# One 64 KB-row load for the keys of two pairs, and the diagonal sums placed behind the next pair's scores, in a one-token decoder block

## The chip, the cores and the metric

The kernel runs on one core of a Trainium2 chip. The metric is the device time of one execution in microseconds (us), the median of several executions. TensorE is called PE, VectorE DVE, ScalarE ACT, GpSimd POOL and SyncE SP, as in the profile.

## What is computed

One token (`x`, 512 wide) goes through a layer-normed attention block over a cache of 16384 keys and values with 8 kv heads, 4 query heads to each, and then through a small mixer and MLP block. Nearly all of the data is the cache: 33.6 MB of keys and as much of values.

```
q = (layernorm(x) @ wq).reshape(32 heads, 128)
scores = einsum("bhqd,bhkd->bhqk", q, repeat(k_cache, 4)) * 128**-0.5
o = einsum("bhqk,bhkd->bhqd", softmax(scores), repeat(v_cache, 4))
h = x + o.reshape(4096) @ wo
...
def B(x):                                  # x = layernorm(h), S = 1
    hs = concat(shifted quarters of gelu(layernorm(x) @ w1)) @ w2
    x1 = x + hs
    return x1 + gelu(layernorm(x1) @ w3) @ w4
return h + B(layernorm(h))
```

With one token, the shifted quarters are all padding, so `hs` is zero and `w1` and `w2` are not read.

## The kernel before

The kv heads are worked in four pairs (`PAIRS`); this text counts them 0 to 3. The 128 partitions hold two heads of 64 rows each, and a partition's part of one pair is 256 keys of 128 numbers, 64 KB. Keys come into `kb`, which holds one pair and has two halves, `kb[0]` and `kb[1]`, of 32 KB per partition (128 keys each). `load_keys(j, y)` loads half `y` of pair `j`. Values come into `vb`, one pair in one load (`load_values`), and `vb` first holds `wq`.

Keys arrive with the head's numbers along the free axis, so DVE transposes each half in 32 x 32 blocks into `kt` (`transpose_keys`, L655). `kt` holds one half, in eight pieces; the `cuts` say at which pieces a transpose begins, so that `(0, 4)` means two transposes of four pieces. PE multiplies the pieces with the query (`scores`, four matmuls per piece, L666) and adds into two PSUM banks. A transpose into a piece of `kt` has to wait until PE has read what half 0 left there.

Then comes `softmax`: the row maximum (`mx`, DVE), its spread over the partitions with a matmul (L683), Exp on ACT, and the transpose of the probabilities to `pt` (L695). In that time `unread(16)` gives PE 16 matmuls whose result nobody reads (L508). `sums` (L713) adds up the denominators, `values` multiplies `pt` with `vb` (L706, 64 matmuls). `gather` takes from its result in `O_ps[0]` the sums that belong to each head (four DVE operations, L722 and L725), a small matmul (L728), and one DVE multiply by the reciprocal denominators into `o_m` (L730). This is called the diagonal sums here. After it, the next pair's query is copied to `qn` (L740) and its keys are transposed.

At the end stand the product with `wo` (L775), the second layer norm, `w3` and `w4` (L828 and L514). `wo` is loaded into `kb[0]`, `w3` and `w4` into `kb[1]`, when the last pair's halves have been read.

Every load but that of `x` goes out on SP's queue, in program order. A load waits on SP until the last readers of its buffer are done. Engines run their own streams; a small planner (`Program`) derives from reads and writes which semaphores each waits for. DVE counts up one semaphore with each operation that is needed elsewhere (a transpose of n pieces counts n), and PE, whose work on the pairs is one loop with registers (`_tensor`), waits for values of that counter. This is why every pair must add the same to it (`worth`, `SEEN`, `ROUND`).

Of the kernel before, what the change touches and what calls it, by code (L numbers as in the profile page):

```python
# [7 lines left out]
BF16 = mybir.dt.bfloat16  # L8
I32 = mybir.dt.int32
# [347 lines left out]
NCH = D // 128  # L357
# [4 lines left out]
WO = ((0, 20), (20, 32))  # L362
VP = 1

SEEN, ROUND = 47, 28
W3 = ((0, 4),)
W4 = ((0, 8), (8, 13), (13, 14))
PAIRS = HKV // 2
RPARTS = 6
QPAD = 4 * 7  # L370
KP = 8 * DH
# [9 lines left out]
def bass_sequential_preLN__gqa_block_cached__mixer_s_mlp__decode_kernel(  # L381
# [13 lines left out]
    with ExitStack() as ctx:  # L395
        sb = lambda name, shape, dt: ctx.enter_context(nc.sbuf_tensor(name, shape, dt))
        ps = lambda name, shape, dt: ctx.enter_context(nc.psum_tensor(name, shape, dt))
        P = Program(nc, ctx)
# [21 lines left out]
        zd = sb("zd", [128, 32], FP32)  # L420
# [9 lines left out]
        nm = sb("nm", [128, 2, REP], FP32)  # L430
        nmh = sb("nmh", [128, 2 * REP], FP32)
        bias = sb("bias", [128, 1], FP32)
# [3 lines left out]
        od = sb("od", [128, 128], FP32)  # L436
        osum = sb("osum", [128, D], FP32)
        den = sb("den", [32, 1], FP32)
# [12 lines left out]
        kb_all = sb("kb", [128, 256 * DH], BF16)  # L451
        kb = [kb_all[:, i * 128 * DH:(i + 1) * 128 * DH] for i in range(2)]
        vb = sb("vb", [128, 256 * DH], BF16)
        kt = sb("kt", [128, 128 * DH], BF16)
        wq_sb, wo_sb = vb, kb[0]
        w3_sb = kb[1][:, 0:NCH * FM].rearrange("p (k f) -> p k f", k=NCH)
        w4_sb = kb[1][:, NCH * FM:2 * NCH * FM].rearrange("p (m c) -> p m c", m=NHC)
# [6 lines left out]
        m_ps, n_ps = mn_ps[:, 0:256], mn_ps[:, 256:512]  # L464


        def load(name, dst, src, key, by="SP", also=()):
            P.op(by, lambda e: e.dma_start(dst, src), w=[key, *also], dma=name)

        def pair_rows(src, j):  # L470
            return src[0, 2 * j:2 * j + 2].rearrange("g (u t) d -> (g u) (t d)", u=64)

        def load_keys(j, y):
            n = 128 * DH
            load(f"k{y}", kb[y][:, :], pair_rows(A_k_cache, j)[:, y * n:(y + 1) * n], ("r", y, 0),
                 also=[("r", y, i) for i in range(1, RPARTS)])

        def load_values(j):
            n = 256 // VP * DH
            if j < PAIRS - 1:  # L480
                load("v", vb[:, :], pair_rows(A_v_cache, j), ("v", 0),
                     also=[("v", x) for x in range(1, VP)] + [("landed", x) for x in range(VP)])
                P.op("POOL", lambda e: e.nop(), r=[("v", 0)], w=[("landed", x) for x in range(VP)],
                     worth=ROUND if j else SEEN, own="v")
                return
            for x in range(VP):
                load(f"v{x}", vb[:, x * n:(x + 1) * n], pair_rows(A_v_cache, j)[:, x * n:(x + 1) * n], ("v", x),
                     also=[("landed", x)])
            for x in range(VP):
                P.op("POOL", lambda e: e.nop(), r=[("v", x)], w=[("landed", x)], worth=ROUND, own="v")  # L490


        def dve(fn, r=(), w=(), bank=(), own=None):
            return P.op("DVE", fn, r, w, bank, own=own)

        def act(fn, r=(), w=(), bank=(), own=None):
            return P.op("ACT", fn, r, w, bank, own=own)
# [4 lines left out]
        def pe(fn, r=(), w=(), bank=(), also=(), times=None, many=1):  # L502

            return P.op("PE", fn, r, w, bank, also=also, times=times, many=many)

        def unread(times):
            field = qb[:, :, :, :].rearrange("p a j q -> p (a j q)")
            P.op("PE", lambda e: e.matmul(O_ps[1][:, :], field[:, 0:128], field[:, 0:512], start=True, stop=True),  # L508
                 r=["qb"], bank=[("O", 1)], times=times)
# [53 lines left out]
        def inverse_roots(i, ns):  # L563
# [36 lines left out]
            r=["ident_f", "x4"], w=["quarter"])  # L600
# [47 lines left out]
                qcol[lo:hi, :, :, 0].rearrange("p n (j h) -> p n j h", h=REP)), r=["qcol"], w=["qb"])  # L648


        def transpose_keys(y, cuts):
            for t, n in zip(cuts, [b - a for a, b in zip(cuts, [*cuts[1:], 8])]):
                view = lambda x, t=t, n=n: x[:, :].bitcast(I32).rearrange("p (x l w) -> p x (l w)", x=2, l=64)[
                    :, :, t * 512:(t + n) * 512]
                P.op("DVE", lambda e, view=view: e.transpose(view(kt), view(kb[y])),  # L655
                     r=[("r", y, i) for i in range(RPARTS)], w=[("kt", t + i) for i in range(n)], worth=n)

        def key_piece(at, n):
            part = kt[:, :].rearrange("p (x f) -> p x f", x=2)[:, :, bass.ds(at, KP)]
# [18 lines left out]
        def softmax(j):  # L678

            dve(lambda e: e.tensor_reduce(mx[:, :], s_all, AX.X, ALU.max), r=[("s", 0), ("s", 1)], w=["mx"], **both)  # L680
            dve(lambda e: e.tensor_scalar(mxd[:, :], ident_f[:, :], mx[:, 0:1], None, ALU.mult),  # L681
                r=["mx", "ident_f"], w=["mxd"])
            pe(lambda e: e.matmul(m_ps[:, 0:128], mean4[:, :], mxd[:, :], start=True, stop=True),  # L683
               r=["mxd", "mean4"], w=["m"], bank=["mn"])
            dve(lambda e: e.tensor_reduce(nm[:, :, :], m_ps[:, 0:128].rearrange("p (g n h) -> p g h n", g=2, h=REP),
                                          AX.X, ALU.min), r=["m"], w=["nm"], bank=["mn"])
            dve(lambda e: e.scalar_tensor_tensor(nmh[:, :], nm[:, :, :].rearrange("p g h -> p (g h)"),  # L687
                                                 32 * D * SCALE, zd[:, :].rearrange("p (n d) -> p n d", d=4)[:, :, 0],
                                                 ALU.mult, ALU.mult, accum_out=bias[:, :]),
                r=["nm", "zd"], w=["nmh", "bias"])  # L690
            act(lambda e: e.activation(p_sb[:, :], s_all, ACTF.Exp, bias=bias[:, 0:1], scale=float(SCALE),  # L691
                                       accum_out=acc[:, :]),
                r=[("s", 0), ("s", 1), "bias"], w=["p", "acc"], **both)
            for g in range(2):
                dve(lambda e, g=g: e.transpose(pt[64 * g:64 * g + 64, :, :, g, :], p_sb[64 * g:64 * g + 64, :]),  # L695
                    r=["p"], w=["pt"])
# [14 lines left out]
        def sums(j):  # L711

            pe(lambda e: e.matmul(n_ps[0:32, 32:33], zd[:, :], acc[:, :], start=True, stop=True),  # L713
               r=["acc", "zd", "pt"], w=["n"], bank=["mn"])
            dve(lambda e: e.reciprocal(den[:, :], n_ps[0:32, 32:33]), r=["n"], w=["den"], bank=["mn"])  # L715
        def gather(j):

            O, key = O_ps[0], ("O", 0)
            for c in range(4):
                block = O[:, c * 128:(c + 1) * 128]  # L720
                if c == 0:
                    dve(lambda e, block=block: e.tensor_scalar(od[:, :], block, rowc[:, 0:1], None, ALU.mult),  # L722
                        r=[key, "rowc"], w=["od"], bank=[key])
                else:
                    dve(lambda e, block=block, c=c: e.scalar_tensor_tensor(  # L725
                        od[:, :], block, rowc[:, c:c + 1], od[:, :], ALU.mult, ALU.add),
                        r=[key, "rowc", "od"], w=["od"], bank=[key])
            pe(lambda e: e.matmul(A_ps[0:32, 0:128], zo[:, :], od[:, :], start=True, stop=True),  # L728
               r=["od", "zo"], w=["A"], bank=["A"])
            dve(lambda e: e.scalar_tensor_tensor(  # L730
                o_m[32 * j:32 * j + 32, :, :], A_ps[0:32, 0:128].rearrange("p (d r) -> p d r", d=4), den[:, 0:1],
                maskdd[0:32, :].unsqueeze(2).to_broadcast([32, 4, 32]), ALU.mult, ALU.mult),
                r=["A", "den", "maskdd"], w=["o_m"], bank=["A"])

        load_values(0)
        for j in range(PAIRS):
            P.part()
            clear()
            P.part("query", j)
            dve(lambda e, j=j: e.tensor_copy(qn[:, :, :], qb[:, :, j, :]), r=["qb", ("s", 0), ("s", 1)], w=["qn"])  # L740
            for y in range(2):
                P.part("half", j, y)
                transpose_keys(y, (0, 4) if j < PAIRS - 1 else range(8) if y else (0, 1, 2, 4, 6))
                scores(j, y)
                if j < PAIRS - 1:
                    load_keys(j + 1, y)
            P.part("middle", j)
            softmax(j)
            unread(16)
            sums(j)  # L750
            values(j)
            P.part("rest", j)
            gather(j)
            if j < PAIRS - 1:
                load_values(j + 1)
        P.part()
        act(lambda e: e.activation(scr[0:1, 1:2], mean4[0:1, 0:1], ACTF.Gelu_apprx_tanh), r=["mean4"], w=["scr"])
        for n, (lo, hi) in enumerate(WO):
# [114 lines left out]
```

## Time and profile before

| | |
|---|---|
| median of 3 runs | 189.70 us (189.63 to 189.85) |
| the profiled execution's own time | 189.84 us |
| its span (first to last instruction) | 188.5 us |
| PE busy | 131.4 us (70%) |
| DVE busy | 116.6 us (62%) |
| ACT busy | 13.7 us (7%) |
| read from HBM | 79.17 MB, 420 GB/s over the span |
| mean granted PE clock | 0.919 |

The profile is one execution. Its span leaves out what lies before the first and after the last instruction, so the execution's own time is 1.34 us longer. A row of the timeline gives start, duration, engine, line, operation and tiles, and in brackets the idle time before it and what ended it. A row of grouped instructions gives, behind the bar, busy time and mean nanoseconds of one. In the view of stretches, the columns are busy time and count by engine, then the granted PE clock as a share, the DMA engines' busy share, and GB/s; packets are counted where they start, so a short stretch can show over 100%.

### The profile page before, as it was taken

To read this page: it belongs to the slowest core of one execution; us is meant where nothing else is said; L and a number is where in the kernel's file an instruction comes from. 1 tells how busy PE (TensorE), PEld (TensorE's weight loads), DVE (VectorE), ACT (ScalarE), POOL (GpSimd) and SP (SyncE) were. 2 spreads that over 40 slices of the span, in tenths; PEclk is the share of its full clock that TensorE was granted. 3 is DMA by queue.
4 is the path that set the end of the run, shared out by engine and by line. 5 is a ranking of instruction groups with operands and counts; after the bars stand their busy time and mean duration, and the time that the engine had idled before them with its cause. 6 is when DMAs were issued, how large, how long until landed. Compare 5 with 4: busy or idle time off the path is not lost.

```text
span 188.5 us, 2406 instructions
## 1 busy us (share of the span) xinstructions
PE 131.4 (70%) x767; PEld 51.1 (27%) x767; DVE 116.6 (62%) x139; ACT 13.7 (7%) x21; POOL 4.6 (2%) x8
## 2 busy tenths in 40 slices
PE   0109902978879419888794198887947999696783
PEld 0103401333324203333242033332422333133321
DVE  5740599699152597891525978915259997543165
ACT  3000100000040000000400000004000000320012
POOL 8100000000000000000000000000000000000000
PEclk9999985599999966999999669999996999999789
DMA  6999999999799999988999999997999999969994
GB/s 227 468 417 445 445 445 445 445 445 445 334 445 445 445 556 417 431 348 382 424 445 445 445 445 445 445 445 341 438 445 445 556 445 431 431 297 404 423 414 162
DMA packets 2895, 79.19 MB, mean 420 GB/s; under 512 B 334, under 2 KB 462, under 8 KB 718
## 3 DMA queue, kind: packets, MB, share of 16 engines
q1 hardware_dynamic: 2886, 79.17, 97.7%
q8 instruction: 1, 0.02, 0.0%
q10 hardware_dynamic: 8, 0.00, 0.0%
HBM read 79.17 MB, written 0.00 MB: 420 GB/s over the span
## 4 chain that ended last, share of the span: by engine, by line
PE 51%; DVE 35%; DMA 6%; issue 6%; ACT 0%; SPq 0%; DVEq 0%; ACTq 0%
DVE kt L655 25%; PE banks L666 20%; PE banks L508 12%; PE banks L706 8%; DMA vb<-in_A_wq_dram 6%; PE banks L632 5%; DVE mx L680 3%; PE banks L775 2%; DVE od L725 2%; PE banks L683 1%; PE banks L728 1%; DVE od L722 1%; DVE qcol L639 1%; DVE mxd L681 1%; PE banks L828 1%
## 5 line engine op out<-in xcount | busy, mean ns | idle before, releaser
L666 PE MATMUL banks<-kt,qn 128*128 x256 | 70.1, 416 | 25.6 <-DVE kt L655 25.4
L655 DVE STREAM_TRANSPOSE kt<-kb 128x4096 int32<-128x4096 int32 (+2 forms) x25 | 70.6, 2878 | 5.2 <-PE banks L666 5.2
L666 PEld LDWEIGHTS banks<-kt,qn 128*128 x256 | 26.2, 102 | 68.9 <-issue 53.5
L508 PE MATMUL banks<-qb 128*128 128x512 bf16 x70 | 25.6, 389 | 0.6
L706 PE MATMUL banks<-vb,pt 128*32 128x512 bf16 x256 | 14.7, 379 | 0.0
L632 PE MATMUL banks<-vb,xn 128*128 x32 | 10.0, 489 | 6.7 <-DVE xn L623 6.7
L691 ACT ACTIVATE p_sb<-banks,bias 128x1024 bf16<-128x1024 f32 x4 | 4.5, 1114 | 132.7 <-DVE nmh L687 132.7
L680 DVE TENSOR_REDUCE mx<-banks 128x1 f32<-128x1024 f32 x4 | 4.9, 1225 | 14.6 <-PE banks L666 14.6
L695 DVE STREAM_TRANSPOSE pt<-p_sb 64x1024 bf16<-64x1024 bf16 x8 | 9.9, 1239 | 5.4 <-ACT p_sb L691 5.3
L508 PEld LDWEIGHTS banks<-qb 128*128 128x128 bf16 x70 | 6.7, 97 | 18.8 <-issue 18.5
L706 PEld LDWEIGHTS banks<-vb,pt 128*32 128x32 bf16 x256 | 9.3, 97 | 3.5
L639 DVE STREAM_TRANSPOSE qcol<-banks 64x1024 f32<-64x1024 f32 x4 | 4.8, 1227 | 8.2 <-PE banks L632 8.2
L722 DVE TENSOR_SCALAR od<-banks,rowc 128x128 f32<-128x128 f32 x4 | 1.4, 350 | 13.4 <-PE banks L706 13.4
L632 PEld LDWEIGHTS banks<-vb,xn 128*128 128x128 bf16 x32 | 3.8, 120 | 12.5 <-issue 10.6
L683 PE MATMUL banks<-mxd,mean 128*128 128x128 f32 x8 | 2.0, 326 | 6.6 <-DVE mxd L681 6.6
L728 PE MATMUL banks<-od,zo 128*32 128x128 f32 x8 | 1.6, 285 | 6.5 <-DVE od L725 6.5
L675 ACT ACTIVATE banks<-mean 128x1024 f32<-128x1024 f32 x4 | 4.1, 1027 | 20.1 <-DVE qcol L639 20.0
L775 PE MATMUL banks<-kb,o_b 128*32 128x512 bf16 x44 | 4.6, 550 | 1.1 <-DVE o_b L771 1.1
L715 DVE RECIPROCAL den<-banks 32x1 f32<-32x1 f32 x4 | 0.6, 155 | 6.9 <-PE banks L713 6.9
L725 DVE SCALAR_TENSOR_TENSOR od<-banks,rowc,od 128x128 f32<-128x128 f32 x12 | 4.2, 351 | 0.4
L601 PE MATMUL banks<-x,quarter 4*128 4x128 bf16 x1 | 0.3, 281 | 5.4 <-DVE quarter L599 5.4
L599 DVE CAST quarter<-ident_f 4x128 bf16<-4x128 f32 x1 | 3.2, 3229 | 1.0 <-DMA x<-in_A_x_dram 1.0
(71 smaller groups left out, 39.9 us busy)
## 6 DMA issues: line engine op xcount, KB each, us to landing
kb<-in_A_k_cache_dram SPq DMA_DIRECT2D x8, 4096.0 KB, 25.5
vb<-in_A_wq_dram SPq DMA_DIRECT2D x1, 3584.0 KB, 11.7
kb<-in_A_wo_dram SPq DMA_DIRECT2D x1, 2560.0 KB, 24.1
kb<-in_B_w_dram SPq DMA_DIRECT2D x1, 1792.0 KB, 23.1
kb<-in_A_wo_dram SPq DMA_DIRECT2D x1, 1536.0 KB, 27.4
kb<-in_B_w_dram SPq DMA_DIRECT2D x1, 1024.0 KB, 25.2
kb<-in_B_w_dram SPq DMA_DIRECT2D x1, 640.0 KB, 26.3
vb<-in_A_wq_dram SPq DMA_DIRECT2D x1, 512.0 KB, 3.7
```

Source lines behind the costliest of these rows:

```text
L508: P.op("PE", lambda e: e.matmul(O_ps[1][:, :], field[:, 0:128], field[:, 0:512], start=True, stop=True), r=["qb"], bank=[("O", 1)], times= ...
L632: pe(lambda e, k=k: e.matmul(row[:, bass.ds(P.b + P.b0, 512)], copies(xn[:, k:k + 1], 128), wq_k[:, k, bass.ds(P.c + P.c0, REP * DH)], sta ...
L639: dve(lambda e, g=g, b=b, half=half: e.transpose(qcol[64 * g:64 * g + 64, 2 * b:2 * b + 2, :, :].rearrange("p e m u -> p (e m u)"), half.r ...
L655: P.op("DVE", lambda e, view=view: e.transpose(view(kt), view(kb[y])), r=[("r", y, i) for i in range(RPARTS)], w=[("kt", t + i) for i in r ...
L666: pe(lambda e, n=n: e.matmul(row[:, bass.ds(P.y, 512)], qn[:, n, bass.ds(P.q, 128)], key_piece(P.k, n), start=False, stop=(n == 3), skip_g ...
L675: act(lambda e: e.activation(s_all, copies(mean4[:, 0:1], 1024), ACTF.Identity, scale=0.0), r=["mean4", "p"], w=[("s", 0), ("s", 1)], **both)
L680: dve(lambda e: e.tensor_reduce(mx[:, :], s_all, AX.X, ALU.max), r=[("s", 0), ("s", 1)], w=["mx"], **both)
L691: act(lambda e: e.activation(p_sb[:, :], s_all, ACTF.Exp, bias=bias[:, 0:1], scale=float(SCALE), accum_out=acc[:, :]), r=[("s", 0), ("s", ...
L695: dve(lambda e, g=g: e.transpose(pt[64 * g:64 * g + 64, :, :, g, :], p_sb[64 * g:64 * g + 64, :]), r=["p"], w=["pt"])
L706: pe(lambda e, l=l, ct=ct, ch=ch: e.matmul(O_ps[0][32 * ct:32 * ct + 32, :], pt[:, l, ch, :, :].rearrange("p g u -> p (g u)"), tiles[:, l ...
L725: dve(lambda e, block=block, c=c: e.scalar_tensor_tensor(od[:, :], block, rowc[:, c:c + 1], od[:, :], ALU.mult, ALU.add), r=[key, "rowc", ...
L775: pe(lambda e, r_=r_, q=q: e.matmul(O_ps[0][32 * q:32 * q + 32, :], copies(o_b[:, r_:r_ + 1], 32), wo_sb[:, r_ * D:(r_ + 1) * D], start=(r ...
```

## The change

- Keys of pairs 1 and 2 (`WHOLE`) come in one load into all of `kb`, with rows of 64 KB, instead of two loads with rows of 32 KB. It is issued where half 1's load was issued. Pairs 0 and 3 keep two loads.
- In pair 1, ACT copies the last three pieces of half 1 (`ASIDE`) to a new buffer, and the transpose of these pieces reads the copy. The load of pair 2's keys then waits for that copy and for DVE's reads up to piece 4 of half 1, not for the last three pieces.
- The diagonal sums of pair j are split in three (`gather`, `rows`, `spread`) and moved behind the scores of pair j + 1: reciprocal and four sums after the last transpose, the matmul before the softmax's, the last multiply after the bias of the Exp. Pair 0 has in their place a memset of `od` and a matmul on it; after the last pair they follow at once.
- 12 unread matmuls per pair instead of 16.
- Pair 3's transposes are cut as (0, 2, 4) and (0, 4, 6, 7), before as (0, 1, 2, 4, 6) and eight single pieces.

```diff
-SEEN, ROUND = 47, 28
+SEEN, ROUND = 53, 28
...
+WHOLE, ASIDE = (1, 2), 3
+LAST = ((0, 2, 4), (0, 4, 6, 7))
...
+        aside = sb("aside", [128, 2, ASIDE * KP], BF16)
...
         def load_keys(j, y):
             n = 128 * DH
+            if j in WHOLE:
+                load("k0", kb_all[:, :], pair_rows(A_k_cache, j), ("r", 0, 0),
+                     also=[("r", 0, i) for i in range(1, RPARTS)] + [("r", 1, i) for i in range(RPARTS)])
+                return
...
+        def pieces(x, t, n):
+            return x[:, :].rearrange("p (x l) -> p x l", x=2)[:, :, t * KP:(t + n) * KP]
+
+        def put_aside():
+            act(lambda e: e.copy(aside[:, :, :], pieces(kb[1], 8 - ASIDE, ASIDE)),
+                r=[("r", 1, i) for i in range(RPARTS)], w=["aside"])
+
-        def transpose_keys(y, cuts):
+        def transpose_keys(y, cuts, from_aside=False):
             for t, n in zip(cuts, [b - a for a, b in zip(cuts, [*cuts[1:], 8])]):
-                view = lambda x, t=t, n=n: x[:, :].bitcast(I32).rearrange("p (x l w) -> p x (l w)", x=2, l=64)[
-                    :, :, t * 512:(t + n) * 512]
-                P.op("DVE", lambda e, view=view: e.transpose(view(kt), view(kb[y])),
-                     r=[("r", y, i) for i in range(RPARTS)], w=[("kt", t + i) for i in range(n)], worth=n)
+                last = from_aside and t == 8 - ASIDE
+                of = aside[:, :, :] if last else pieces(kb[y], t, n)
+                P.op("DVE", lambda e, of=of, t=t, n=n: e.transpose(pieces(kt, t, n).bitcast(I32), of.bitcast(I32)),
+                     r=["aside"] if last else [("r", y, i) for i in range(RPARTS)],
+                     w=[("kt", t + i) for i in range(n)], worth=n)
...
-                r=["nm", "zd"], w=["nmh", "bias"])
+                r=["nm", "zd"], w=["nmh", "bias"], worth=1 + (j == 0))
+            spread(j - 1)
...
-            dve(lambda e: e.reciprocal(den[:, :], n_ps[0:32, 32:33]), r=["n"], w=["den"], bank=["mn"])
-        def gather(j):
-
-            O, key = O_ps[0], ("O", 0)
+
+        def gather(j):
+
+            O, key = O_ps[0], ("O", 0)
+            P.part("late", j)
+            if j < 0:
+                P.op("DVE", lambda e: e.memset(od[:, :], 0.0), w=["od"], worth=1 + NCH)
+                return
+            dve(lambda e: e.reciprocal(den[:, :], n_ps[0:32, 32:33]), r=["n"], w=["den"], bank=["mn"])
...
+        def rows(j):
             pe(lambda e: e.matmul(A_ps[0:32, 0:128], zo[:, :], od[:, :], start=True, stop=True),
                r=["od", "zo"], w=["A"], bank=["A"])
+
+        def spread(j):
+            if j < 0:
+                P.count["DVE"] += 1
+                return
             dve(lambda e: e.scalar_tensor_tensor(
...
+            if j == WHOLE[0]:
+                put_aside()
             for y in range(2):
                 P.part("half", j, y)
-                transpose_keys(y, (0, 4) if j < PAIRS - 1 else range(8) if y else (0, 1, 2, 4, 6))
+                if j == WHOLE[0] and y:
+                    transpose_keys(y, (0, 4, 8 - ASIDE), from_aside=True)
+                else:
+                    transpose_keys(y, LAST[y] if j == PAIRS - 1 else (0, 4))
                 scores(j, y)
-                if j < PAIRS - 1:
+                if j < PAIRS - 1 and (y or j + 1 not in WHOLE):
                     load_keys(j + 1, y)
+            gather(j - 1)
             P.part("middle", j)
+            rows(j - 1)
             softmax(j)
-            unread(16)
+            unread(12)
             sums(j)
             values(j)
-            P.part("rest", j)
-            gather(j)
             if j < PAIRS - 1:
                 load_values(j + 1)
+        P.part()
+        gather(PAIRS - 1)
+        P.part()
+        rows(PAIRS - 1)
+        spread(PAIRS - 1)
```

More of the change, by code (lines that the diff above doesn't have):

```diff
@@ L686, in softmax @@
                                           AX.X, ALU.min), r=["m"], w=["nm"], bank=["mn"])
-            dve(lambda e: e.scalar_tensor_tensor(nmh[:, :], nm[:, :, :].rearrange("p g h -> p (g h)"),
+            P.op("DVE", lambda e: e.scalar_tensor_tensor(nmh[:, :], nm[:, :, :].rearrange("p g h -> p (g h)"),
                                                  32 * D * SCALE, zd[:, :].rearrange("p (n d) -> p n d", d=4)[:, :, 0],
                                                  ALU.mult, ALU.mult, accum_out=bias[:, :]),
-                r=["nm", "zd"], w=["nmh", "bias"])
+                r=["nm", "zd"], w=["nmh", "bias"], worth=1 + (j == 0))
+            spread(j - 1)
             act(lambda e: e.activation(p_sb[:, :], s_all, ACTF.Exp, bias=bias[:, 0:1], scale=float(SCALE),
```

## The prediction

> **What bounds the kernel now.** I read the page first, its slices and its DMA queues.
>
> ```profile
> span 188.5 us, 2406 instructions
> DMA  6999999999799999988999999997999999969994
> ...
> q1 hardware_dynamic: 2886, 79.17, 97.7%
> ```
>
> The 16 DMA engines are busy nearly all the time: 97.7% of the span on the one queue that carries every load. The few lower digits are slices into which fewer packet starts fell. So the loads are one stream, and the bytes are not changed. I then set each load's place in that stream from SyncE's timeline (when it was issued) and from the DMA view of a small window around the issue (how long until it landed).
>
> ```profile
> 0.73 0.87 SPq L468 DMA_DIRECT2D vb<-in_A_wq_dram  x2
> ...
> 36.23 11.07 SPq L468 DMA_DIRECT2D kb<-in_A_k_cache_dram  x2
> 63.07 0.33 SPq L468 DMA_DIRECT2D vb<-in_A_v_cache_dram  x1
> 74.35 10.79 SPq L468 DMA_DIRECT2D kb<-in_A_k_cache_dram  x2
> ...
> 112.13 10.67 SPq L468 DMA_DIRECT2D kb<-in_A_k_cache_dram  x2
> 138.42 0.33 SPq L468 DMA_DIRECT2D vb<-in_A_v_cache_dram  x1
> ...
> 159.02 1.75 SPq L468 DMA_DIRECT2D kb<-in_B_w_dram  x4
> ```
>
> The DMA view of the windows at 46.0, 63.0, 84.0, 122.0, 138.0 and 158.0 us, in this order:
>
> ```profile
> kb<-in_A_k_cache_dram SPq DMA_DIRECT2D x1, 4096.0 KB, 24.1
> ...
> vb<-in_A_v_cache_dram SPq DMA_DIRECT2D x1, 27.4
> ...
> kb<-in_A_k_cache_dram SPq DMA_DIRECT2D x1, 4096.0 KB, 25.1
> ...
> kb<-in_A_k_cache_dram SPq DMA_DIRECT2D x1, 4096.0 KB, 26.2
> ...
> vb<-in_A_v_cache_dram SPq DMA_DIRECT2D x1, 29.6
> ...
> kb<-in_B_w_dram SPq DMA_DIRECT2D x1, 128.0 KB, 26.1
> ```
>
> A row with x2 spans two issues; the second begins some 0.33 us before its end. I count the pairs of kv heads from 0 to 3. So pair 1's second half of keys lands at 46.97 + 24.1 = 71.1, pair 1's values at 63.07 + 27.4 = 90.5, pair 2's second half at 84.8 + 25.1 = 109.9, pair 3's at 122.5 + 26.2 = 148.7, pair 3's values at 138.42 + 29.6 = 168.0, and the last piece of w4 at 160.4 + 26.1 = 186.5. Each of these is issued 24 us or more before it lands, far ahead of its own transfer: the queue never runs dry.
>
> Beside the stream stands a second chain, of VectorE (DVE) and TensorE (PE), which the timeline shows without a pause from pair to pair:
>
> ```profile
> 27.39 8.77 DVE L655 STREAM_TRANSPOSE kt<-kb 128x4096 int32<-128x4096 int32 x2
> ...
> 51.23 1.23 DVE L680 TENSOR_REDUCE mx<-banks 128x1 f32<-128x1024 f32 x1 [4.34 <-PE banks L666]
> ...
> 65.30 0.30 DVE L740 COPY qn<-qb 128x624 bf16<-128x624 bf16 x1
> 65.53 8.75 DVE L655 STREAM_TRANSPOSE kt<-kb 128x4096 int32<-128x4096 int32 x2
> 70.12 9.19 PE L666 MATMUL banks<-kt,qn 128*128 x32 [5.13 <-DVE kt L655]
> 75.97 8.77 DVE L655 STREAM_TRANSPOSE kt<-kb 128x4096 int32<-128x4096 int32 x2 [1.69 <-PE banks L666]
> ...
> 89.05 1.23 DVE L680 TENSOR_REDUCE mx<-banks 128x1 f32<-128x1024 f32 x1 [4.31 <-PE banks L666]
> ...
> 90.98 5.98 PE L508 MATMUL banks<-qb 128*128 128x512 bf16 x16
> ...
> 93.02 2.49 DVE L695 STREAM_TRANSPOSE pt<-p_sb 64x1024 bf16<-64x1024 bf16 x2 [1.33 <-ACT p_sb L691]
> ...
> 100.67 0.35 DVE L722 TENSOR_SCALAR od<-banks,rowc 128x128 f32<-128x128 f32 x1 [3.35 <-PE banks L706]
> ...
> 103.29 8.76 DVE L655 STREAM_TRANSPOSE kt<-kb 128x4096 int32<-128x4096 int32 x2
> ...
> 126.70 1.23 DVE L680 TENSOR_REDUCE mx<-banks 128x1 f32<-128x1024 f32 x1 [4.30 <-PE banks L666]
> ```
>
> Read pair 1: transposes from 65.53, the row maximum at 89.05, the probabilities transposed by 95.51 (93.02 + 2.49), the 16 filler matmuls until 96.96, the values until 100.6, the diagonal sums from 100.67, pair 2's transposes from 103.29. One pair takes 103.29 − 65.53 = 37.8 us, and the stream needs about 38.8 for its 16.8 MB (71.1 to 109.9). The two run side by side, and the end shows which is later:
>
> ```profile
> 152.42 8.16 PE L666 MATMUL banks<-kt,qn 128*128 x32 [0.24 <-DVE kt L655]
> ...
> 160.61 1.22 DVE L680 TENSOR_REDUCE mx<-banks 128x1 f32<-128x1024 f32 x1 [1.67 <-PE banks L666]
> ...
> 168.53 0.19 PE L713 MATMUL banks<-acc,zd 128*32 128x1 f32 x1
> ...
> 186.80 0.23 PE L514 MATMUL banks<-kb,hcol 128*32 128x128 bf16 x4
> ```
>
> The last matmuls (L514) start at 186.80, and their weights were there at 186.5. So compute ends the kernel, but only 0.3 us behind the stream. No saving in compute can bring more than these 0.3 us and what the stream itself gains.
>
> **The change, part by part.** *Rows of 64 KB.* The DMA view of a window with value packets alone (33 to 47 us, 64 KB each) and of one with key packets (13 to 30 us: 224 of 32 KB and 16 tiny ones):
>
> ```profile
> q1 hardware_dynamic: 96, 6.29, 103.7%
> ...
> q1 hardware_dynamic: 240, 7.34, 100.0%
> ```
>
> A 64 KB packet takes 1.037 × 14 × 16 / 96 = 2.420 us, a 32 KB one 17 × 16 / 224 = 1.214; twice that is 2.428. An engine moves 8 rows of 64 KB per pair, so a pair gains 8 × 0.009 = 0.07 us, the two pairs 0.14. All later landings come 0.14 earlier.
>
> *What the one load takes away.* Half 0 of pair 1 could be read before half 1 had come; now nothing of pair 1 can be read before the whole has landed, at 71.1 − 0.07 = 71.0. Pair 1 then starts at about 71.1 instead of 65.53 (0.1 us for the handover; between DVE and PE it is at most 70.12 − 65.53 − 4.38 = 0.2). Pair 2 starts at 109.9 − 0.14 + 0.1 = 109.9 instead of 103.29. That is 6.6 us given away, which the rest has to bring back.
>
> *Issue of the two loads.* Pair 1's goes out when pair 0's half 1 is transposed, at 47.0 as the second half does now; its turn comes when pair 0's values have landed, 71.1 − 19.4 = 51.7 (half of the 38.8 us for half of a pair's bytes), some 4 us later. Pair 2's has to wait for all reads of kb in pair 1: DVE's up to piece 4 of half 1, and ScalarE's copy of the last three pieces. From the start at 71.1: half 1 begins 75.97 − 65.53 = 10.44 later, four pieces take 8.77 / 2 = 4.38, one piece 1.21:
>
> ```profile
> L655 DVE STREAM_TRANSPOSE kt<-kb 128x1024 int32<-128x1024 int32 x10 | 11.5, 1210 | 0.0
> ...
> L675 ACT ACTIVATE banks<-mean 128x1024 f32<-128x1024 f32 x4 | 4.1, 1027 | 20.1 <-DVE qcol L639 20.0
> ...
> L803 ACT ACTIVATE xs<-hr,st 128x128 f32<-128x128 f32 x1 | 0.4, 385 | 0.0
> ```
>
> That makes 87.1. The copy has 6144 elements per partition; ScalarE's slope between the two rows is (1.027 − 0.385) / 896 = 0.72 ns an element, so 4.7 us, at most 6.2 by the larger row alone: done by 77.3, while its reader comes at 87.1. It costs nothing; without that cover it would cost those 5 us. When must the load be there? From a first issue to its first packet, and how far the engines stand apart (windows 1.2 to 2 us and 84 to 86 us, 40 slots each):
>
> ```profile
> DMA  0000000000000000000000010005699059909905
> ...
> DMA  0000000000009990999909090000000000000000
> ```
>
> The load issued at 0.73 has its first packets at slot 28 of 0.02 us, 1.76: 1.03 us. The engines' starts lie within 14 slots of 0.05, some 0.7, and I take 1. Pair 1's values land at 90.4, so the first engine is free at about 89.4 and the issue has until 88.3. It comes at 87.1: a margin of 1.2 us, no gap.
>
> *Diagonal sums behind the next scores.* Now DVE's chain has, from 100.67 to 103.29, 2.6 us of sums and query copy after the values. Moved, the reciprocal and the four sums run between the last transposes and the row maximum, where DVE waits 4.3 us for PE; PE's small matmul runs beside the maximum; the last multiply runs beside Exp, where DVE waits 1.33. Each is covered; uncovered the whole would cost about 2.4 us per pair. Better: the next query copy and transposes no longer wait for the values at all. They start when the probabilities are transposed.
>
> *12 fillers instead of 16.* Four fewer at 5.98 / 16 = 0.37 bring PE's readiness from 96.96 to 95.46, and the probabilities are there at 95.51: now these decide, a gain of some 1.3 us.
>
> *The sum.* Start to maximum took 23.84, 23.52 and 23.41 us in pairs 0 to 2; mean 23.6. Pair 2: 109.9 + 23.6 = 133.5; probabilities transposed 95.51 − 89.05 = 6.46 later, 139.95; query copy 0.25, so pair 3's transposes start at 140.2. Half 0 takes 8.75: 148.95. Half 1 has landed (148.5); its first four pieces are ready at 153.3, and with 0.2 for the handover its scores start at 153.5, against 152.42. They take 160.61 − 152.42 = 8.19: maximum at 161.7, 1.1 later than before. The new cuts in pair 3 keep PE busy, so only this start counts. Then 6.46 + 0.1: sums and values at 168.3, against 168.53. Pair 3's values are there at 167.9. So compute gains 0.2 us, and the end follows it: 186.6 for L514, where the weights allow 186.4. The profiled execution took 189.84 for a span of 188.5, 1.34 around it, and lies 0.14 above the median of 189.70. On the median the gain of 0.2 gives **189.5 us**.
>
> **One number that no row fixes: PE's cold start.** PE will stand idle from the end of pair 1's values (71.1 + 23.6 + 6.6 + 3.7 = 105.0) to pair 2's scores (109.9 + 4.6 = 114.5), 9.5 us; before pair 1's scores it was 5.13.
>
> ```profile
> 70.12:73.94 3.82, 3.82 (x9) 1.38 (x10) 3.82 (x1) 0.00 (x0) 0.00 (x0) 0.50 1.23 532
> ```
>
> At the start of pair 1's scores the granted clock is 0.50, and nine matmuls take 3.82 / 9 = 0.424 us each. The first 16 took 75.97 − 70.12 = 5.85 there; all 16 at half clock would take 6.8. This is the bound above: 0.95 more in pair 2, whose half 1 waits for these 16. The bound below is the stream: 0.4 in all.
>
> The Trainium skill (TensorE: Matmul & The Clock Gate, Part 1: The HAM clock gate) says that an idle PE falls to half clock and that this lasts until a busy stretch of about 3.4 us has filled a window that runs freely, wherever the first matmul falls in it. By that rule the slow stretch could be anything from 3.4 to 6.8 us, and the sum by it would lie between the stream's floor of 189.3 and 190.4; the trace's 0.50 and 3.82 us agree with the half clock, and no run here shows how the phase moves when the idle time changes.
>
> **Rivals.** *Stream-bound (faster).* The slow stretch in pair 2 is shorter than in pairs 0 to 2, or a handover is; then L514 starts when w4 is there, at 186.4. Gain 0.4: 189.3. For: only 0.2 us away from the sum. Against: the three pairs differ by 0.4 among themselves, no more. *Cold PE (slower).* All 16 first matmuls of pair 2 at half clock: +0.95, 190.4. It makes the kernel slower by over 0.2% from +0.6 on. For: the idle time before them nearly doubles; of the three pairs, start to maximum, none is a sure guide for it. The same in pair 1 takes the issue of pair 2's keys to 88.1, 0.2 short of the limit; beyond it each us is a us of gap. *PE late in pair 3 (slower).* Half 1's first transpose overwrites what half 0's first four pieces read. PE comes from the values of pair 2 at 133.5 + 6.5 + 3.7 = 143.7 and needs 4.1 for them (half of 8.16), 147.8, against 148.95. The margin is 1.1; at half clock they would take 6.8, 1.5 us late: 191.0. Against: values run just before. *Rows still moved in 32 KB packets.* Then the 0.14 are missing at pair 2's start: 189.6.
>
> **How the numbers follow.** A measurement of this kernel can tell about 0.2%, 0.38 us, from no change. Forecast 0.43 (189.35 to 190.0, within 0.2%); 32 KB packets 0.03 (within); stream-bound 0.24 (189.3, faster by just over 0.2%); cold PE 0.22 and PE late 0.08 (slower). So faster 0.24, same 0.46, slower 0.30. The range goes from just under the stream's floor, 189.25, to just over the cold case, 190.5; beyond lie a gap in the stream and the late PE.
>
> **What would show it.** Right: two key issues fewer, landings 0.1 earlier from pair 3 on, no gap between values and keys at 89 to 90 us; pair 1's transposes from 71.1 and pair 2's from 109.9; pair 2's key issue near 87.1; sums ahead of each maximum with no wait behind them; pair 3's transposes near 140.2 and its maximum near 161.7; values of pair 3 near 168.3. Wrong: the 5.85 of the first 16 matmuls grown past 6.5, pair 3's half 1 waiting for PE, or a last w4 landing later than 186.5.

## The result: 0.7% slower, and the profile after

The changed kernel takes 1.0069 times as long as the kernel before (95% interval 1.0056 to 1.0083); on 189.68 us, the median of 22 runs of before, that is 1.3 us. The changed kernel's own 22 runs go from 189.38 to 193.39 with a median of 191.29; the kernel before stays between 189.50 and 190.35. The ratio leaves out runs more than 1.5% above the fastest of their kernel, so it lies below the ratio of the medians. The forecast was no change, 189.5, in a range that ended at 190.5.

The profiled execution took 191.34. From its page, the span, the slices, the load queue and the chain that ended last:

```profile
span 190.0 us, 2341 instructions
...
DMA  6999999999999999999799999999999999989993
...
q1 hardware_dynamic: 2598, 79.17, 97.3%
...
DMA 46%; DVE 29%; PE 17%; issue 6%; ACT 1%; SPq 1%; DVEq 0%; ACTq 0%
```

The same bytes, and the engines look about as busy as before: 97.3% of a span that is 1.5 us longer. So the transfers themselves have become longer, on the mean of the engines by 0.7 us: 97.7% of 188.5 was 184.2 us, 97.3% of 190.0 is 184.9. The chain now goes through DMA for 46% of the span. Its last part in order of time shows where:

```profile
87.39 24.28 DMA kb<-in_A_k_cache_dram
...
111.77 4.46 DVE kt L669
...
116.39 5.83 PE banks L681 x16
...
160.64 27.27 DMA kb<-in_B_w_dram
187.91 0.04 issue
187.95 0.46 PE banks L866 x20
188.41 0.11 PE banks L521 x4
```

Pair 2's keys are issued at 87.39, 0.3 us later than the forecast 87.1, and land 24.28 us later, at 111.7. With a stream that ran on they would have been there at 109.8. Their transposes start at 111.77. The last weights are issued with the last of these four and land by the DMA view of that window:

```profile
159.78 1.80 SPq L471 DMA_DIRECT2D kb<-in_B_w_dram  x4
...
kb<-in_B_w_dram SPq DMA_DIRECT2D x1, 128.0 KB, 27.1
```

That is 161.2 + 27.1 = 188.3 instead of 186.4. From DVE's and PE's timelines:

```profile
71.14 8.77 DVE L669 STREAM_TRANSPOSE kt<-kb 128x4096 int32<-128x4096 int32 x2 [13.99 <-DMA kb<-in_A_k_cache_dram]
...
111.77 8.77 DVE L669 STREAM_TRANSPOSE kt<-kb 128x4096 int32<-128x4096 int32 x2 [10.34 <-DMA kb<-in_A_k_cache_dram]
...
131.40 1.12 DVE L746 SCALAR_TENSOR_TENSOR od<-banks,rowc,od 128x128 f32<-128x128 f32 x3
135.38 1.23 DVE L695 TENSOR_REDUCE mx<-banks 128x1 f32<-128x1024 f32 x1 [2.87 <-PE banks L681]
...
142.11 17.60 DVE L669 STREAM_TRANSPOSE kt<-kb 128x2048 int32<-128x2048 int32 x7
...
163.68 1.22 DVE L695 TENSOR_REDUCE mx<-banks 128x1 f32<-128x1024 f32 x1 [2.52 <-PE banks L681]
...
170.19 0.19 PE L729 MATMUL banks<-acc,zd 128*32 128x1 f32 x1
...
188.28 0.22 PE L521 MATMUL banks<-kb,hcol 128*32 128x128 bf16 x4
```

Pair 1 starts at 71.14 (forecast 71.1). Pair 2 starts 1.9 us later than forecast, and everything behind it is late by the same: pair 3's transposes 142.11 against 140.2, its maximum 163.68 against 161.7, its sums 170.19 against 168.3. The diagonal sums are covered: DVE still waits 2.87 and 2.52 us for PE behind them. So what remains to explain is one load that came 1.9 us late although it was issued 2 us ahead of its turn.

How the load begins is seen in the DMA view of the 2 us from 89.4 to 91.4, 40 slots of 0.05 us; a digit stands where packets start. First the changed kernel, then the same kernel in another execution, which took 189.44; below each row the packets that start in the window, their MB, and the time that they take, as a share of 16 engines' 2 us:

```profile
DMA  0999999099009900000090000000000009000000
...
q1 hardware_dynamic: 30, 0.98, 138.9%
```

```profile
DMA  0009999999900000000000000000000000000000
...
q1 hardware_dynamic: 32, 1.05, 121.4%
```

In the good execution all 16 engines begin the load between slots 3 and 10, from 89.55 to 89.95. In the bad one the starts are strewn to slot 33, 91.05, 3.7 us after the issue. Half of the counted packets are tiny. The 15 large ones of the bad execution take 2.96 us each (138.9% of 32 us, divided by 15; the sixteenth began just before the window), the 16 of the good one 2.43.

The packets and the semaphore counts in the two traces tell the rest. In the bad execution the rows that begin before 94 us take 2.4 to 4.0 us, those that begin later 2.42 as in the good one. The lag that the engines have by then stays: they finish pair 2's keys between 109.76 and 111.67, and the last weights between 186.45 and 188.24. In the good execution they finish them between 109.30 and 109.61, and between 185.92 and 186.25.

### The profile page after: what moved, and what is told of

Same layout as the page of the kernel before. It is cut to its first block, busy times and chain, and to the rows that moved or that the text cites. A ratio compares the mean times of both kernels' runs of the same rounds, so it can differ in the third digit from the quotient of the medians.

```text
span 190.0 us, 2341 instructions
## 1 busy us (share of the span) xinstructions
PE 122.2 (64%) x753; PEld 49.1 (26%) x753; DVE 116.0 (61%) x135; ACT 19.0 (10%) x22; POOL 4.6 (2%) x8
## 3 DMA queue, kind: packets, MB, share of 16 engines
q1 hardware_dynamic: 2598, 79.17, 97.3%
## 4 chain that ended last, share of the span: by engine, by line
DMA 46%; DVE 29%; PE 17%; issue 6%; ACT 1%; SPq 1%; DVEq 0%; ACTq 0%
DMA kb<-in_A_k_cache_dram 26%; DVE kt L669 26%; DMA kb<-in_B_w_dram 14%; PE banks L681 11%; DMA vb<-in_A_wq_dram 6%; PE banks L639 5%; DVE pt L711 1%; DVE qcol L646 1%; DVE mx L695 1%; ACT p_sb L707 1%; SPq L471 1%; DVE qb L653 0%; PE banks L698 0%; PE banks L866 0%; DVE qn L768 0%
## 5 line engine op out<-in xcount | busy, mean ns | idle before, releaser
L681 PE MATMUL banks<-kt,qn 128*128 x256 | 68.2, 409 | 41.6 <-DVE kt L669 41.2
L669 DVE STREAM_TRANSPOSE kt<-kb 128x4096 int32<-128x4096 int32 (+2 forms) x19 | 67.0, 3575 | 29.6 <-DMA kb<-in_A_k_cache_dram 24.3
L515 PE MATMUL banks<-qb 128*128 128x512 bf16 x54 | 19.3, 388 | 0.5
L639 PE MATMUL banks<-vb,xn 128*128 x32 | 9.3, 464 | 6.8 <-DVE xn L630 6.8
L515 PEld LDWEIGHTS banks<-qb 128*128 128x128 bf16 x54 | 5.2, 98 | 13.5 <-issue 13.3
L662 ACT COPY aside<-kb 128x6144 bf16<-128x6144 bf16 x1 | 5.3, 5312 | 15.7 <-DMA kb<-in_A_k_cache_dram 15.7
L690 ACT ACTIVATE banks<-mean 128x1024 f32<-128x1024 f32 x4 | 4.1, 1027 | 19.4 <-DVE qcol L646 19.3
L813 PE MATMUL banks<-kb,o_b 128*32 128x512 bf16 x44 | 3.4, 384 | 1.2 <-DVE o_b L809 1.1
L669 DVE STREAM_TRANSPOSE kt<-aside 128x3072 int32<-128x3072 int32 x1 | 3.3, 3334 | 0.0
```

The lines of the kernel that those rows point to most:

```text
L639: pe(lambda e, k=k: e.matmul(row[:, bass.ds(P.b + P.b0, 512)], copies(xn[:, k:k + 1], 128), wq_k[:, k, bass.ds(P.c + P.c0, REP * DH)], sta ...
L662: act(lambda e: e.copy(aside[:, :, :], pieces(kb[1], 8 - ASIDE, ASIDE)), r=[("r", 1, i) for i in range(RPARTS)], w=["aside"])
L669: P.op("DVE", lambda e, of=of, t=t, n=n: e.transpose(pieces(kt, t, n).bitcast(I32), of.bitcast(I32)), r=["aside"] if last else [("r", y, i ...
L681: pe(lambda e, n=n: e.matmul(row[:, bass.ds(P.y, 512)], qn[:, n, bass.ds(P.q, 128)], key_piece(P.k, n), start=False, stop=(n == 3), skip_g ...
L690: act(lambda e: e.activation(s_all, copies(mean4[:, 0:1], 1024), ACTF.Identity, scale=0.0), r=["mean4", "p"], w=[("s", 0), ("s", 1)], **both)
```

## The experiments

Two theories stood against each other at first. *Lead*: a load that is issued too shortly before its turn in the stream begins raggedly. *Shape and neighbours*: this load is slow because of its 64 KB rows in one piece, or because of the copy and the transposes beside it. The prediction's own rival, PE's cold start, was the third.

### More and fewer pieces aside

The copy aside is what sets the issue time of pair 2's keys. With four pieces the load need not wait for the fifth piece's transpose, with two it waits for one transpose more:

```diff
-WHOLE, ASIDE = (1, 2), 3
+WHOLE, ASIDE = (1, 2), 4
...
-                    transpose_keys(y, (0, 4, 8 - ASIDE), from_aside=True)
+                    transpose_keys(y, (0, 8 - ASIDE), from_aside=True)
```

> The changed kernel with four pieces of half 1 copied aside instead of three, so that the load of pair 2's keys is issued one piece (some 1.2 us) earlier, about 3.2 us before its turn instead of 2.0. Theory of the lead (a load issued too shortly before its turn in the stream runs its first packets slowly on every engine, and each engine keeps its lag to the end): first packets at about normal length, keys of pair 2 there at about 109.8 instead of 111.7, last piece of w4 at 186.4, time about 189.4 with little spread. Rival (the load is slowed by its shape or by what runs beside it, ScalarE's copy and the transposes): the copy only grows, so 191 again or more. Rival of PE's cold start: nothing changes, 190 to 192 with the same spread.

> The changed kernel with two pieces aside: the load of pair 2's keys is issued about 1.2 us later, some 0.9 us before its turn. Theory of the lead: the lag grows by about the 1.1 us, pair 2's keys there near 112.8, time about 192.2. Rival of shape and neighbours: less is copied, so 190.5 to 191. Rival of the cold start: 191 as before.

Four pieces: ratio to before 1.0015 (0.9999 to 1.0030), median 189.85; two: 1.0090 (1.0066 to 1.0115), median 191.28. SyncE's row of the issue, the landing in the DMA view around it, and the starts from 89.4 on; four pieces, then two:

```profile
86.65 0.33 SPq L471 DMA_DIRECT2D kb<-in_A_k_cache_dram  x1
...
kb<-in_A_k_cache_dram SPq DMA_DIRECT2D x1, 23.2
...
DMA  9999999990000000000000000000000000000000
```

```profile
88.50 0.33 SPq L471 DMA_DIRECT2D kb<-in_A_k_cache_dram  x1
...
kb<-in_A_k_cache_dram SPq DMA_DIRECT2D x1, 22.7
...
DMA  0000909999999900000009009000090000000000
```

With the issue at 86.65 the keys land at 109.85, where the forecast had them, and the starts stand close. The load has the same shape and the copy beside it is larger: shape and neighbours fall. But the lead theory in its simple form missed, too: the issue at 88.50 was expected to cost 1.1 us more than the one at 87.39, and costs about the same; the keys land at 111.2. And three of the twelve runs with four pieces took 190.7 to 190.8, so the lead of 2.8 us in this trace is not always enough.

### One part at a time

`WHOLE = (1,)` takes pair 2's keys in two halves again, without a copy aside; `WHOLE = ()` takes all in halves and keeps the moved sums, 12 fillers and new cuts; and the kernel before with the whole loads and the copy alone is the other half of the change.

> The changed kernel with one load for the keys of pair 1 only; pair 2's come as two loads again, without a copy aside, the first issued after half 0 of pair 1, 9 us before its turn. Theory of the lead: no slow packets, time about 189.4 with little spread. Rival of the shape: the slow packets go with the 64 KB rows of this load, so 189.4 as well, but then the kernel before with late issue stays at 189.7. Rival of the cold start: 190 to 191 and the same spread.

> The changed kernel without any one-piece load: all keys in halves, diagonal sums behind the next scores, 12 fillers, the new cuts. Issues 9 us or more ahead of their turns. Theory of the lead: no slow packets; compute is far ahead, so the stream sets the end: 0.07 us later than with one whole load, 189.6, within 0.1 of the kernel before less 0.3 for the last matmuls, so 189.4 to 189.6. Rival (the moved sums or the fewer fillers are what costs): 190.5 or more, with the spread of the changed kernel.

> The kernel before with only the loads of the change: keys of pairs 1 and 2 in one load each, three pieces aside; sums, 16 fillers and cuts as before. Pair 2 cannot start before 109.9 to 111.7 and pair 3 only a whole pair later (37.7 us), at 147.6 to 149.4 instead of 140.75; the rest is as before. Theory of the lead and rivals alike: 6.9 to 8.7 us longer, 196.5 to 198.5, less some tenths for PE that starts warmer or colder. If it were much less, the sums' move would not be what pays for the whole loads.

Pair 1 alone in one load: 0.9994 (0.9986 to 1.0003), median 189.55. None: 0.9997 (0.9988 to 1.0006), median 189.60. So moved sums, fillers and cuts cost nothing that can be measured, nor does the 64 KB load that is issued early; but they do not bring a measurable gain either, as the stream then sets the end (in both traces PE waits for the last weights). Whole loads alone: 1.0396 (1.0367 to 1.0424), median 197.0, 7.5 us, within the forecast. DVE's timeline of that kernel:

```profile
110.44 8.77 DVE L668 STREAM_TRANSPOSE kt<-kb 128x4096 int32<-128x4096 int32 x2 [1.19 <-DMA kb<-in_A_k_cache_dram]
...
147.77 17.96 DVE L668 STREAM_TRANSPOSE kt<-kb 128x1024 int32<-128x1024 int32 x13
```

Pair 2 waits for its keys until 110.44, and pair 3 starts at 147.77 instead of 140.99. These 6.8 us are close to the 6.6 that the prediction booked as given away. In the changed kernel pair 3 starts at 142.11, in its good execution at 139.68, so the moved sums and fewer fillers bring nearly all of it back. The issue of pair 2's keys, and their landing by the DMA view around it:

```profile
87.71 0.33 SPq L470 DMA_DIRECT2D kb<-in_A_k_cache_dram  x1
...
kb<-in_A_k_cache_dram SPq DMA_DIRECT2D x1, 22.6
```

In this trace the first engine ends the load ahead at 89.91, so the lead is 2.2 us, hardly longer than in the changed kernel. Yet the keys are there at 110.3, only 0.3 us later than 19.4 us behind the values, which landed at 90.6. This execution went nearly free as well.

### The issue held back

To have the lead alone, a load was held back by ScalarE operations that write a buffer of their own. The first attempt put such an operation into the kernel before, behind the last transpose of pair 1.

> The kernel before, with both half loads of pair 2's keys held back by a ScalarE operation of some 2.5 us after the last transpose of pair 1, so that the first is issued near 87.4, 2 us before its turn. Rows stay 32 KB, nothing is copied from kb, nothing else is moved. Theory of the lead: the first packets of this load run long, the landings from there on are 1 to 2 us later, and the time is 190.5 to 191.5. Rival of shape and neighbours: no slow packets, 189.7. Rival of the cold start: 189.7.

It missed its aim: the whole chain ran earlier in the profiled execution, and the issue came at 85.11, with 4 us and more to spare.

```profile
85.11 0.80 SPq L469 DMA_DIRECT2D kb<-in_A_k_cache_dram  x2
```

1.0009 (0.9998 to 1.0020) says nothing on a short lead; two of the ten runs took 190.2 and 190.5, and when they issued the load is not known. In the kernel with one whole load the transposes start when the keys of pair 1 land, so the time of issue is steady. There pair 2's first half load, 4 MB with 32 KB rows, is free to go at 79.91; two operations after half 0's last transpose hold it back:

```diff
+                if j == 1 and not y:
+                    for _ in range(2):
+                        act(lambda e: e.activation(lag[:, :], copies(mean4[:, 0:1], 4250), ACTF.Identity),
+                            r=["mean4", ("kt", 7), "lag"], w=["lag"])
+                    load_keys(j + 1, y, ["lag"])
```

> The kernel with one load for pair 1's keys only (pair 2's as two loads of 32 KB rows, no copy aside), and the first of pair 2's loads held back by two ScalarE operations of 3.7 us after half 0's last transpose, so that it is issued near 87.4, 2 us before its turn at 89.5, instead of 9.6 us before. Nothing reads kb beside it that did not before. Theory of the lead: first packets run long, engines fall 1 to 2 us apart, last landing near 188, time 190.5 to 191.5. Rival of the shape (only the 8 MB load with 64 KB rows, or its copy, is slow): 189.5 as without the hold.

> As the held-back kernel, with two shorter ScalarE operations (2.7 us each): pair 2's first load is issued near 85.4, 4 us before its turn. Theory of the lead: by then all engines have their first rows before the stream reaches them, no long packets, 189.5 to 189.7. Rival (the hold itself costs, whatever the lead, for instance by ScalarE's work beside): 191 again.

> The same with a hold that leaves about 3 us. Theory of the lead with a limit between 2 and 3 us: mostly 189.6, a few executions up to 190.5. If the limit is higher, 190 to 191.

> The same with a hold that leaves about 0.9 us. Theory of the lead as one us lost for each us missing: 192 to 193. If instead every load that comes short of the limit loses about the same, as two pieces aside against three suggest: 191 to 192.

The hold does more than set this issue. Its operations read the last piece of `kt`, so pair 1's second transpose of half 1, which overwrites that piece, has to wait for them, and with it all that follows, up to the load of pair 2's values. DVE and SyncE with 4250 elements held, SyncE with 4900, and SyncE without a hold:

```profile
87.64 4.45 DVE L670 STREAM_TRANSPOSE kt<-kb 128x4096 int32<-128x4096 int32 x1 [1.95 <-ACT lag L781]
...
107.94 0.33 SPq L472 DMA_DIRECT2D vb<-in_A_v_cache_dram  x1
```

```profile
110.20 0.33 SPq L472 DMA_DIRECT2D vb<-in_A_v_cache_dram  x1
```

```profile
104.48 0.33 SPq L471 DMA_DIRECT2D vb<-in_A_v_cache_dram  x1
```

The turn of these values comes at about 109.2, when the first engine has moved its last keys. So with 4250 elements a second load has a short lead, 1.3 us; with 4900 it is issued after most engines have run out of work, and its first row begins at 111.17.

The lead is counted to 89.5, where the stream reaches the first half of pair 2's keys in these traces. Issue, landing and the issue of the values come from one traced execution each; at 3650, 4250 and 4900 that was the slowest of its kernel (190.89, 192.71 and 192.47):

| elements held | issue | lead | first half lands | values issued | median | runs | ratio to before (95%) |
|---|---|---|---|---|---|---|---|
| none | 79.91 | 9.6 | 100.0 | 104.48 | 189.55 | 12 | 0.9994 (0.9986 to 1.0003) |
| 3080 | 85.61 | 3.9 | 100.2 | 105.62 | 189.61 | 10 | 1.0000 (0.9991 to 1.0010) |
| 3650 | 86.71 | 2.8 | 101.4 | 106.26 | 189.88 | 12 | 1.0000 (0.9984 to 1.0016) |
| 4250 | 87.53 | 2.0 | 101.3 | 107.94 | 191.49 | 5 | 1.0093 (1.0062 to 1.0123) |
| 4900 | 88.63 | 0.9 | 100.9 | 110.20 | 192.11 | 4 | 1.0121 (1.0105 to 1.0136) |

Issue and starts, for 3080 elements and for 4250:

```profile
85.61 5.74 SPq L472 DMA_DIRECT2D kb<-in_A_k_cache_dram  x2
...
DMA  0999999990009000000000000999999990009000
```

```profile
87.53 4.91 SPq L472 DMA_DIRECT2D kb<-in_A_k_cache_dram  x2
...
DMA  0999909900009000000990000999909909000900
```

In the first, the pattern of the starts comes again unchanged 24 slots later, with the second row of 32 KB (1.2 us). In the second it is torn: single engines begin at slots 19 and 20, and the second rows follow as unevenly. So a short lead is enough for ragged starts and a late landing, with rows of either size, in one piece or two, with a copy or without: the first half lands at 101.3 instead of 100.0, long before the values are issued.

The medians of the last two rows are not the price of this one lead, though. By the traces the second half of the keys lands at 111.2 and 110.7 instead of 109.8, but the values at 132.4 and 132.0 instead of 129.1: 1.9 us of each loss are added by the values' late issue. What the lead alone costs is seen more cleanly with more and fewer pieces aside, where the values are issued at 105.5 and 105.0, more than 3 us ahead of their turn.

### The same kernel again

> The changed kernel once more, for a second trace. Theory of the lead: again an issue of pair 2's keys near 87.4 with long first packets behind it and engines that end 1 to 2 us apart; if this execution happens to issue it before 86.7, little of that and a time near 189.5. Rival of PE's cold start: the time follows the length of the first 16 matmuls of pair 2, not the landings.

> The changed kernel a third time, for its trace. Issue near 87.4 again. Theory of the lead: the time follows the last landing of pair 2's keys; about 191 with a landing near 111, 189.4 with one near 109.7. Theory of PE's cold start: the time follows the scores of pair 2.

They took 189.44 and 191.06. The first, by SyncE, the DMA view of its issue and the timelines:

```profile
87.60 0.33 SPq L471 DMA_DIRECT2D kb<-in_A_k_cache_dram  x1
...
kb<-in_A_k_cache_dram SPq DMA_DIRECT2D x1, 22.0
...
109.70 8.77 DVE L669 STREAM_TRANSPOSE kt<-kb 128x4096 int32<-128x4096 int32 x2 [8.07 <-DMA kb<-in_A_k_cache_dram]
...
132.96 1.23 DVE L695 TENSOR_REDUCE mx<-banks 128x1 f32<-128x1024 f32 x1 [2.86 <-PE banks L681]
...
139.68 17.69 DVE L669 STREAM_TRANSPOSE kt<-kb 128x2048 int32<-128x2048 int32 x7
...
161.34 1.23 DVE L695 TENSOR_REDUCE mx<-banks 128x1 f32<-128x1024 f32 x1 [2.53 <-PE banks L681]
...
186.29 0.22 PE L521 MATMUL banks<-kb,hcol 128*32 128x128 bf16 x4
```

The second:

```profile
87.30 0.33 SPq L471 DMA_DIRECT2D kb<-in_A_k_cache_dram  x1
...
kb<-in_A_k_cache_dram SPq DMA_DIRECT2D x1, 24.1
...
111.48 8.77 DVE L669 STREAM_TRANSPOSE kt<-kb 128x4096 int32<-128x4096 int32 x2 [10.14 <-DMA kb<-in_A_k_cache_dram]
...
135.19 1.23 DVE L695 TENSOR_REDUCE mx<-banks 128x1 f32<-128x1024 f32 x1 [2.87 <-PE banks L681]
```

The time follows the landing: 109.6, 111.4 and, in the first trace, 111.7 go with 189.44, 191.06 and 191.34. PE's part differs by less: from pair 2's start to its maximum the three took 23.26, 23.71 and 23.61 us.

But the lead is about 2 us in all three, and one lost nothing. One idea was left for that: in the good execution the issue came just after all engines had begun their last packet of the load ahead. So three more holds, of 4340, 4450 and 4580 elements, put the issue there.

> The held-back kernel with the issue of pair 2's first load some 1.85 us ahead of its turn, near 87.7, when the engines have just begun their last packets of the load ahead. If the lead alone decides: 191.5 to 191.8, between the holds that left 2.0 and 0.9 us. If the place among the packets decides: 189.6 to 190.3.

> The same with 1.65 us, near 87.9, clearly behind all starts of the last packets. If the lead alone decides: 191.6 to 191.9. If the place among the packets decides: 189.6 to 190.

> The same with 1.4 us, near 88.1. If the lead alone decides: 191.8 to 192. If the place among the packets decides: 190 or less, with what the last engines then wait for their rows.

SyncE's rows of the three:

```profile
87.78 4.91 SPq L472 DMA_DIRECT2D kb<-in_A_k_cache_dram  x2
```

```profile
87.79 4.91 SPq L472 DMA_DIRECT2D kb<-in_A_k_cache_dram  x2
```

```profile
87.95 4.91 SPq L472 DMA_DIRECT2D kb<-in_A_k_cache_dram  x2
```

The second came out at the issue time of the first. 1.0077 (1.0059 to 1.0096), 1.0093 (1.0076 to 1.0109) and 1.0149 (1.0132 to 1.0166), medians 191.32, 191.59 and 192.60, the last above both of its forecasts. These medians, too, hold values that were issued late, at 108.1 to 108.3. But the first half of the keys by itself lands at 102.3, 102.1 and 102.6 in the three traces, over 2 us behind the 100.0 without a hold: the idea falls.

Of the changed kernel's 22 runs, one lost nothing and the others lie 0.5 to 3.7 us above the 189.68 of before; with two pieces aside, 1 us ahead, the four runs lie 1.1 to 2.5 us above theirs. How much is lost is not read off the lead alone, and why single executions go free stays open. No variant went below the kernel before by more than can be measured.

## Why the prediction was wrong

*The step that failed* is "a margin of 1.2 us, no gap", in the issue of the two loads. It took 1.03 us, the time from the kernel's first issue to its first packet, for the time that a load needs ahead of its turn. That number fits the first engine (with two pieces aside, issued at 88.50, the first row begins in slot 4, at 89.6, 1.1 us later) and says nothing of the other fifteen: in the trace after, an engine begins its rows as late as 3.7 us after the issue. The spread of the engines, taken as 1 us, was read between 84 and 86 us, in the middle of a load that had been issued at 63.07, and not at the start of one. The issue came 0.3 us later than forecast, but by this reckoning a margin of 0.9 us was left. The runs put the needed lead between 2.0 us (the changed kernel, 1.0069) and 3.9 us (1.0000); at 2.8, with four pieces aside or 3650 elements held, 20 of 24 runs lie within 0.4 us of before. The case stood in the text only as "beyond lie a gap in the stream", outside the range, with no chance of its own, and its price was set at each us missing, though what happens is not a gap of that length.

The Trainium skill (DMA: Bandwidth & Descriptors, Specifications) gives about 0.6 us to the first byte for loads issued from SyncE. By that figure the margin would have seemed larger still; the first load here shows 1.03 for its first packet, and neither number tells when the last engine begins.

*The stream.* The prediction had it end 0.2 us ahead of compute and never run dry, and the consequence was not drawn: a late engine has no slack in which to catch up. The last engine's 1.9 us at pair 2's keys is still there at the last weights, 188.3 against 186.4.

*The rest of the sum* can be read from the execution that lost nothing. Pair 2's start 109.70 (forecast 109.9), its maximum 132.96 (133.5), pair 3's transposes 139.68 (140.2), its maximum 161.34 (161.7), the last matmuls 186.29 (186.6, floor 186.4), the time 189.44 (189.5). The cover of the sums, ScalarE's copy, the 12 fillers and the later start of PE in pair 3 were sized well; the copy took 5.3 us, between the 4.7 and 6.2 given. The slow execution agrees from its later start on: pair 3's transposes begin 6.7 us after pair 2's maximum (forecast 6.7) and its maximum comes 21.6 us later (21.5). So the sum holds for an even stream; that one execution met 189.5 says nothing for the forecast of the median.

*The rivals.* The stream-bound case cannot be told from the sum in the good execution: 189.44 lies between 189.3 and 189.5, and its timeline shows no wait of the last matmuls for the weights. The cold PE did not come: 23.3 to 23.7 from pair 2's start to its maximum, against 23.6, and in the first trace the first 16 matmuls took 5.83, where the prediction set 6.5 as the sign. PE late in pair 3 did not come either. The 0.07 us per pair for 64 KB rows cannot be told from nothing in the times (189.55 and 189.60 with and without).

## What to carry to other kernels

In a kernel that a stream of loads bounds, ask of each load how long before its turn it is issued, and keep 3 to 4 us for this kind of load (2.8 was mostly enough here, 3.9 in all ten runs); find the smallest lead that the present kernel lives with, and treat less than that as unknown, not as a margin. The latency of the first packet is not the latency of the load. What is saved by fewer and longer loads (here an estimated 0.07 us a pair) must be weighed against the buffer time they need, as a whole buffer comes free later than its half.

## What the runs showed of the hardware beyond what was expected

A load that is issued 2 us before its turn keeps the queue busy by the page (97.3%) and still loses 1.6 and 1.9 us in two of three traces, in ragged starts and long first packets (2.96 us against 2.43) rather than in a hole that the page shows. An engine's lag then stays to the end of the kernel: the engines are 1.9 us apart at pair 2's keys and 1.8 at the last weights, 77 us later. And a lead of 2.0 us is no sharp limit: the same kernel with the same issue time took 189.4 once and 191 in other executions, so that its 22 runs spread over 4 us where the 22 of the kernel before, run with them, spread over 0.9 (among 21 others of the kernel before, one took 191.15).
